# Gated recurrence and max-out MoE on one core: the orders of units 1 and 2 redrawn, the small sums first, one hid group ahead of the state's output

## Chip, core and metric

The kernel runs on one core of a Trainium2 chip. The metric is the device time of an execution in microseconds (us); smaller is better. Nine runs of the kernel before gave a median of 156.73 us, from 155.72 to 158.37.

## What is computed

Two layers follow each other. The first is a gated linear recurrence for each batch b and head h, with a 48 x 48 state that decays by alpha along its rows; the second is a max-out MLP on the recurrence's output, with all heads of a token side by side.

```python
# B, H, S, D = 4, 8, 768, 48
state = zeros((B, H, D, D))
for t in range(S):
    state = alpha[:, :, t, :, None] * state + einsum('bhd,bhe->bhde', k[:, :, t], v[:, :, t])
    y[:, :, t] = einsum('bhd,bhde->bhe', q[:, :, t], state)

x = y.transpose(0, 2, 1, 3).reshape(B * S, H * D)      # 3072 x 384
g = maximum(x @ w1, x @ w2)                            # 3072 x 1024
out = g @ w_out                                        # 3072 x 384
```

## The kernel before

**Units.** Time is cut into six chunks of 128 steps, and the four batches into two pairs. A unit u is one chunk of one pair, so there are 12 units; u and u-2 are neighbours in time for the same batches. Each unit has two halves, bb = 0 and 1, one for each batch of its pair.

**The recurrence of a unit.** Within a chunk the recurrence is done with matmuls. With L the running sum of log alpha in the chunk, counted from its middle:

- `ln(u)` takes the logarithm of alpha on ScalarE (ACT, L160) into `lg`.
- `sums(u)` adds up on TensorE: four matmuls against a triangular mask `mc` (L181, 384 columns, each on 64 rows, that is K=64) give L for both halves in two PSUM tiles `cs`; eight small matmuls against `halves` (L184, 4 columns, on 128 rows) give `dps`, the sums over the halves of the chunk, in spare columns of the first `cs` tile.
- `expm`, `expp` and `expd` (together `exps`) are ACT's exponentials: exp(-L) into `Em` (L197), exp(L) in place (L202), the chunk's decay `de` (L207).
- `kmul` makes k exp(-L) on GpSimd (POOL, L232), `qmul` makes q exp(L) on VectorE (DVE, L236, `qn`), `vcast` casts v to 16 bits on POOL (L169). `scale(u, bb)` is these three for one half.
- `turn(u, bb)` transposes kn and qn of one half on TensorE (L243) and copies them out on DVE (L245, `qk`).
- `kv(u)` is the chunk's own state (L259), added on DVE to the carried state `sb` into `tm` (L267; L269 for the first chunk); `state(u)` decays `tm` of unit u-2 into `sb` on POOL.
- `pairs(u, bb)` multiplies q with k of one half (L279, on 48 rows), and DVE applies the triangular mask while it copies out (L281, `pt`): two instructions for each half, called masks below.
- For units 0 and 1, whose carried state is zero, `yfirst` makes the output of one half (L327), evicted on ACT (`xn`, L333), and `xfirst` transposes it (L340) and copies it out on DVE (`xt`, L341). From unit 2 on `ystate` adds the part from the carried state (L291, 16 matmuls on 48 rows), `yin` the part within the chunk (L303), and `xturn` transposes.

**The MLP of a unit.** `hid(u, f2)` is one of four groups of six matmuls of 256 columns (L352); its relu into `gT` is done by ACT (L357), for the last group by DVE (L359). The weights are prepared so that w2's part goes straight to the output: `outp(u, n)` has three matmuls against `w2o` (L368) and eight against `w_out` (L370) for one half, an eviction on ACT (L373), and after both halves an output DMA issued by ACT (L378).

**Order.** The order of the calls is written out by hand under a manual schedule: each engine runs its instructions in the order of the Python calls. The first two units are written out one by one (from L424); from unit 2 on, a loop (from L509) interleaves unit u's recurrence, unit u-1's MLP and the preparation of unit u+1. `dummies(n)` are n matmuls on zeros (L416) whose result is not used.

**Buffers and loads.** PSUM has four tiles of tag `g`, two of `m` (hid, outp, dummies) and two of `pp` (pairs). Inputs have four buffers each and are loaded by SyncE (SP), in the order of the calls `load(u)`: two DMAs for alpha (L68) and three for k, q and v (L80). ACT's output DMAs share the DMA engines with these loads.

Of the kernel before, what the change touches and what calls it, by code (L numbers as in the profile page):

```python
# [15 lines left out]
def kernel(  # L16
# [22 lines left out]
    nc = tc.nc  # L39
    B, H, S, D = q.shape  # L40
# [69 lines left out]
    mc = constp.tile([128, 2, C], FP16)  # L110
    nc.gpsimd.memset(mc, 1.0)
    for bb in range(2):
        r = slice(64 * bb, 64 * bb + 64)
# [5 lines left out]
        r = slice(64 * bb, 64 * bb + 32)  # L119
# [30 lines left out]
    def pair(t, j):  # L150
        return t[:, 2 * j : 2 * j + 2, :].rearrange("p h w -> p (h w)")
# [5 lines left out]
    def ln(u):  # L157
        X = st[u]
        X["lg"] = LG[u % NB]
        nc.scalar.activation(  # L160
            out=X["lg"][:, :, :, 0:D], in_=X["af"].rearrange("p h j d -> p j h d"), func=ACTF.Ln
        )

    def vcast(u, bbs=(0, 1)):
        X = st[u]
        if 0 in bbs:
            X["v16"] = gp.tile([128, 2, H, D], FP16, tag="v16", name="v16")
        e = slice(bbs[0], bbs[-1] + 1)
        nc.gpsimd.tensor_copy(out=X["v16"][:, e], in_=X["vf"][:, e])  # L169

    def sums(u):
        X = st[u]
        c, g = divmod(u, NG)
        lg = X["lg"]
        cs = [new("g", [128, 512], FP32, 4, "cs") for _ in range(2)]
        X["csv"] = csv = [x[:, 0 : H * D].rearrange("p (h d) -> p h d", h=H) for x in cs]
        dps = cs[0][:, H * D : H * D + 4 * HP].rearrange("p (j b n) -> p j b n", j=HP, b=2)
        for j in range(2):
            for bb in range(2):
                r = slice(64 * bb, 64 * bb + 64)  # L180
                nc.tensor.matmul(csv[bb], lhsT=mc[r, j], rhs=lg[r, j, :, 0:D], start=(j == 0), stop=(j == 1))  # L181
        for hp in range(HP):
            for j in range(2):
                nc.tensor.matmul(  # L184
                    dps[:, hp], lhsT=pair(lg[:, j], hp), rhs=halves, start=(j == 0), stop=(j == 1)
                )
        X["dps"] = dps
        X["qn"], X["kn"], X["Em"] = [], [], []
        for bb in range(2):
            X["qn"].append(QN[(2 * u + bb) % (2 * NB)])  # L190
            X["kn"].append(KN[(2 * u + bb) % (2 * NB)])
# [7 lines left out]
    def expp(u, bb):  # L199

        X = st[u]
        nc.scalar.activation(out=X["csv"][bb], in_=X["csv"][bb], func=ACTF.Exp)  # L202
# [6 lines left out]
    def exps(u):  # L209
        for bb in range(2):  # L210
            expm(u, bb)
            expp(u, bb)
        expd(u)
# [24 lines left out]
    def turn(u, bb):  # L238
        X = st[u]
        tp = new("g", [128, 2, HP, C], FP16, 4, "tp")  # L240
        for n, src in ((1, X["kn"][bb]), (0, X["qn"][bb])):
            for j in range(HP):
                nc.tensor.transpose(tp[:, n, j, :], pair(src, j), ident)  # L243
        qk = gp.tile([128, 2, HP, C], FP16, tag="qk", name="qk")
        nc.vector.tensor_copy(out=qk, in_=tp)  # L245
        X["qk", bb] = qk
# [24 lines left out]
    def pairs(u, bb):  # L271
        X = st[u]
        qk = X["qk", bb]
        pt = X["pt", bb] = gp.tile([128, 2, HP, C], FP16, tag="pt", name="pt")
        pa = [new("pp", [128, HP, C], FP32, 2, "pp") for _ in range(2)]
        for j in range(HP):
            for a in range(2):
                r = slice(64 * a, 64 * a + D)
                nc.tensor.matmul(pa[a][:, j, :], lhsT=qk[r, 1, j, :], rhs=qk[r, 0, j, :], start=True, stop=True)  # L279
        for a in range(2):  # L280
            nc.vector.tensor_mul(out=pt[:, a], in0=pa[a], in1=u16.unsqueeze(1).to_broadcast([128, HP, C]))  # L281

    def ystate(u):
        X = st[u]
        X["ya"] = ya = [new("g", [128, 2, HP, D], FP32, 4, "ya") for _ in range(2)]
        X["begun"] = begun = set()
        for bb in range(2):
            for j in range(HP):
                for a in range(2):
                    r = slice(64 * a, 64 * a + D)  # L290
                    nc.tensor.matmul(  # L291
                        ya[a][:, bb, j, :], lhsT=X["qk", bb][r, 0, j, :], rhs=X["sb"][r, bb, j, :],
                        start=a not in begun, stop=False,
                    )
                    begun.add(a)
# [39 lines left out]
    def xfirst(u, bb):  # L335
        X = st[u]
        xp = new("g", [128, ND, C], FP16, 4, "xb")
        xf = X["xn"][:, bb].rearrange("p j a d -> p (j a d)")
        for ds in range(ND):
            nc.tensor.transpose(xp[:, ds, :], xf[:, ds * 128 : (ds + 1) * 128], ident)  # L340
        nc.vector.tensor_copy(out=X["xt"][:, :, bb, :], in_=xp)  # L341

    def hid(u, f2):
        X = st[u]
        if f2 == 0:
            X["gT"] = mp.tile([128, NF, 2 * C], FP16, tag="gT", name="gT")
        gT = X["gT"]
        hp = new("m", [128, 2, 2 * C], FP32, 2, "hp")
        for n in range(2):
            f = 2 * f2 + n  # L350
            for ds in range(ND):
                nc.tensor.matmul(  # L352
                    hp[:, n, :], lhsT=w12[:, ds, f * 128 : (f + 1) * 128],
                    rhs=X["xt"][:, ds].rearrange("p n t -> p (n t)"), start=(ds == 0), stop=(ds == ND - 1),
                )
        if f2 != 3:
            nc.scalar.activation(out=gT[:, 2 * f2 : 2 * f2 + 2, :], in_=hp, func=ACTF.Relu)  # L357
        else:
            nc.vector.tensor_relu(out=gT[:, 2 * f2 : 2 * f2 + 2, :], in_=hp)  # L359

    def outp(u, n):
        X = st[u]
        c, g = divmod(u, NG)
        if n == 0:
            X["outs"] = mp.tile([128, 2, DM], FP32, tag="outs", bufs=2, name="outs")
        op = new("m", [128, DM], FP32, 2, "op")
        for ds in range(ND):
            nc.tensor.matmul(op, lhsT=X["xt"][:, ds, n, :], rhs=w2o[:, ds, :], start=(ds == 0), stop=False)  # L368
        for f in range(NF):
            nc.tensor.matmul(  # L370
                op, lhsT=X["gT"][:, f, n * C : (n + 1) * C], rhs=wo16[:, f, :], start=False, stop=(f == NF - 1)
            )
        nc.scalar.copy(out=X["outs"][:, n, :], in_=op)  # L373
        dst = out.rearrange("(b s) d -> s b d", b=B)[c * C : (c + 1) * C, 2 * g : 2 * g + 2, :]
        if u == NU - 1:
            nc.scalar.dma_start(out=dst[:, n], in_=X["outs"][:, n])
        elif n == 1:
            nc.scalar.dma_start(out=dst, in_=X["outs"])  # L378
# [34 lines left out]
    def dummies(n):  # L413
        warm = new("m", [128, 512], FP32, 2, "warm")
        for _ in range(n):
            nc.tensor.matmul(warm, lhsT=wz[:, 0:128], rhs=wz, start=True, stop=True)  # L416

    def scale(u, bb):
        kmul(u, bb)
        qmul(u, bb)  # L420
        vcast(u, (bb,))
# [49 lines left out]
    hid(0, 2)  # L471
    expm(1, 1)
    expp(1, 1)
    hid(0, 3)
    expd(1)
    scale(1, 0)
    outp(0, 0)
    turn(1, 0)
    kv(1, (0,))
    outp(0, 1)  # L480
    pairs(1, 0)
    load(4)
    scale(1, 1)
    turn(1, 1)
    kv(1, (1,))
    yfirst(1, 0)
    dummies(1)
    pairs(1, 1)
    xfirst(1, 0)
    ln(2)  # L490
    dummies(2)
    yfirst(1, 1)
    sums(2)
    exps(2)
    xfirst(1, 1)
    for bb in range(2):
        kmul(2, bb)
    state(2)
    for f2 in range(4):
        hid(1, f2)  # L500
    for bb in range(2):
        qmul(2, bb)
    vcast(2)
    load(5)
    turn(2, 0)
    turn(2, 1)


    for u in range(2, NU):  # L509
        nxt = u + 1 < NU  # L510
        pairs(u, 0)
        kv(u)
        if nxt:
            ln(u + 1)
        if u > 2:
            hid(u - 1, 0)
            hid(u - 1, 1)
        else:
            outp(1, 0)
        if nxt:  # L520
            sums(u + 1)
            exps(u + 1)
            for bb in range(2):
                kmul(u + 1, bb)
            state(u + 1)
            vcast(u + 1)
        pairs(u, 1)
        ystate(u)
        if u > 2:
            hid(u - 1, 2)  # L530
            hid(u - 1, 3)
        if nxt:
            for bb in range(2):
                qmul(u + 1, bb)
        yin(u)
        outp(u - 1, 0 if u > 2 else 1)
        if nxt:
            turn(u + 1, 0)
        xturn(u)
        if nxt:  # L540
            turn(u + 1, 1)
        if u > 2:
            outp(u - 1, 1)
        if u + 4 < NU:
            load(u + 4)
# [34 lines left out]
```

## Time and profile before

| | |
|---|---|
| median of nine runs | 156.73 us |
| the profiled execution | 157.22 us, of it a span of 155.5 us |
| TensorE: busy with matmuls | 139.9 us (90% of the span), 1670 matmuls |
| VectorE | 93.0 us (60%) |
| ScalarE | 78.7 us (51%) |
| GpSimd | 47.4 us (30%) |
| DMA | 28.58 MB, mean 184 GB/s |
| granted TensorE clock | 1.000 |

The span runs from the first to the last instruction of the program; what the execution takes beyond it, 1.7 us, lies around the program. The chain that ended last puts 67% of the span on TensorE and 13% on SP's queue, the latter all in the first 21 us. In the loop one step takes about 10.15 us: sums of successive units start at 68.35, 78.51, 88.66 and so on.

How to read rows: a row of the timeline has start, duration, engine, line, operation, tiles and how many instructions it merges, and in brackets how long the engine was idle before it and what ended that. Rows of the chain have start, duration and place. A row of waits has the total in us, how often, and the longest. TensorE's instructions name the rows and columns of the array that they use, so 64*128 is on 64 rows.

### The profile page before, as it was taken

To read this page: it belongs to the slowest core of one execution; us is meant where nothing else is said; L and a number is where in the kernel's file an instruction comes from. 1 tells how busy PE (TensorE), PEld (TensorE's weight loads), DVE (VectorE), ACT (ScalarE), POOL (GpSimd) and SP (SyncE) were. 2 spreads that over 40 slices of the span, in tenths; PEclk is the share of its full clock that TensorE was granted. 3 is DMA by queue.
4 is the path that set the end of the run, shared out by engine and by line. 5 is a ranking of instruction groups with operands and counts; after the bars stand their busy time and mean duration, and the time that the engine had idled before them with its cause. 6 is when DMAs were issued, how large, how long until landed. Compare 5 with 4: busy or idle time off the path is not lost.

```text
span 155.5 us, 4085 instructions
## 1 busy us (share of the span) xinstructions
PE 139.9 (90%) x1670; PEld 96.4 (62%) x1670; DVE 93.0 (60%) x192; ACT 78.7 (51%) x165; POOL 47.4 (30%) x73
## 2 busy tenths in 40 slices
PE   6778868795769898999999999999999999999991
PEld 2236344563455577777777677786776777777660
DVE  5057814648449588676687684967867665654010
ACT  3375235813552668176293582853917629344421
POOL 6032320240260717209045081270530903500000
PEclk9999999999999999999999999999999999999999
DMA  3999999899999998999989999989989842020202
GB/s 85 195 383 212 364 220 315 153 202 241 202 187 185 189 222 191 194 232 195 201 213 199 188 243 212 190 205 201 242 168 210 208 90 103 4 101 0 94 11 101
DMA packets 93459, 28.58 MB, mean 184 GB/s; under 512 B 87424, under 2 KB 93056, under 8 KB 93440
## 3 DMA queue, kind: packets, MB, share of 16 engines
q1 hardware_dynamic: 90160, 23.60, 83.8%
q10 hardware_dynamic: 3280, 4.72, 8.8%
q8 instruction: 13, 0.21, 0.6%
q14 instruction: 6, 0.05, 0.1%
HBM read 23.59 MB, written 4.72 MB: 182 GB/s over the span
## 4 chain that ended last, share of the span: by engine, by line
PE 67%; SPq 13%; DVE 6%; ACT 5%; DMA 5%; issue 2%; ACTq 1%; DVEq 0%
PE op L370 20%; PE hp L352 16%; PE op L368 8%; PE tp L243 6%; SPq L80 5%; DMA w1f<-in_moe_w_dram 5%; PE pp L279 4%; SPq L103 3%; DVE pt L281 3%; PE kv L259 2%; PE ya L303 2%; PE cs L181 2%; PE xp L318 2%; SPq L68 2%; PE ya L291 2%
## 5 line engine op out<-in xcount | busy, mean ns | idle before, releaser
L232 POOL TENSOR_TENSOR kn<-kf,Em 128x384 f16<-128x384 f32 x24 | 23.6, 1001 | 77.4 <-ACT Em L197 65.7
L281 DVE TENSOR_TENSOR pt<-pp,u 128x512 f16<-128x512 f32 x48 | 30.9, 685 | 13.5 <-PE pp L279 12.6
L352 PE MATMUL hp<-xt,w 128*128 128x256 f16 x288 | 35.9, 273 | 2.2 <-DVE w L409 1.1
L370 PE MATMUL op<-wo,gT 128*128 128x384 f16 x192 | 35.1, 326 | 0.0
L373 ACT COPY outs<-op 128x384 f32<-128x384 f32 x24 | 11.5, 478 | 42.8 <-PE op L370 42.8
L352 PEld LDWEIGHTS <-w 128*128 128x128 f16 x288 | 26.5, 98 | 7.0 <-DVE w L409 2.1
L370 PEld LDWEIGHTS <-gT 128*128 128x128 f16 x192 | 18.8, 98 | 12.4
L245 DVE COPY qk<-tp 128x1024 f16<-128x1024 f16 x24 | 16.4, 687 | 12.7 <-PE tp L243 12.7
L357 ACT ACTIVATE gT<-hp 128x512 f16<-128x512 f32 x36 | 20.5, 594 | 4.5 <-PE hp L352 4.1
L359 DVE TENSOR_SCALAR gT<-hp 128x512 f16<-128x512 f32 x12 | 8.3, 692 | 12.7 <-PE hp L352 12.7
L236 DVE TENSOR_TENSOR qn<-qf,cs 128x384 f16<-128x384 f32 x24 | 12.3, 547 | 6.0 <-ACT de L207 6.0
L368 PE MATMUL op<-w2o,xt 128*128 128x384 f16 x72 | 15.6, 325 | 0.1
L160 ACT ACTIVATE lg<-af 128x768 f16<-128x768 f32 x12 | 10.1, 843 | 10.6 <-DMA af<-in_alpha_dram 6.9
L416 PE MATMUL warm<-wz 128*128 128x512 f16 x38 | 12.1, 446 | 1.3 <-DVE halves L123 1.3
L197 ACT ACTIVATE Em<-cs 128x384 f32<-128x384 f32 x24 | 11.7, 487 | 1.9 <-PE cs L184 1.7
L243 PE MATMUL tp<-ident,qn 128*128 128x128 f16 x96 | 9.3, 220 | 3.5 <-DVE qn L236 3.5
L202 ACT ACTIVATE cs<-cs 128x384 f32<-128x384 f32 x24 | 11.8, 490 | 0.0
L267 DVE TENSOR_TENSOR tm<-kv,sb 64x192 f32<-64x192 f32 x32 | 11.3, 352 | 0.5
L169 POOL CAST v<-vf 128x768 f16<-128x768 f32 (+1 forms) x14 | 10.2, 731 | 2.7 <-DMA vf<-in_v_dram 2.7
L279 PE MATMUL pp<-qk 48*128 48x128 f16 x192 | 9.6, 219 | 0.7 <-DVE qk L245 0.7
L243 PE MATMUL tp<-ident,kn 128*128 128x128 f16 x96 | 9.3, 220 | 0.3 <-POOL kn L232 0.3
L310 ACT CAST xn<-ya 128x384 f16<-128x384 f32 x20 | 8.6, 484 | 1.2 <-PE ya L303 0.7
(57 smaller groups left out, 140.9 us busy)
## 6 DMA issues: line engine op xcount, KB each, us to landing
af<-in_alpha_dram SPq DMA_DIRECT2D x24, 192.0 KB, 5.8
out_dram<-outs ACTq DMA_DIRECT2D x11, 384.0 KB, 4.9
kf<-in_k_dram SPq DMA_DIRECT2D x10, 384.0 KB, 6.2
qf<-in_q_dram SPq DMA_DIRECT2D x10, 384.0 KB, 7.5
vf<-in_v_dram SPq DMA_DIRECT2D x10, 384.0 KB, 6.6
w2f<-in_moe_w_dram SPq DMA_DIRECT2D x3, 512.0 KB, 5.3
wof<-in_moe_w_out_dram SPq DMA_DIRECT2D x2, 768.0 KB, 7.4
w1f<-in_moe_w_dram SPq DMA_DIRECT2D x4, 384.0 KB, 9.5
```

Source lines behind the costliest of these rows:

```text
L202: nc.scalar.activation(out=X["csv"][bb], in_=X["csv"][bb], func=ACTF.Exp)
L232: nc.gpsimd.tensor_mul(out=X["kn"][bb][:, :, 0:D], in0=X["kf"][:, bb], in1=X["Em"][bb])
L236: nc.vector.tensor_mul(out=X["qn"][bb][:, :, 0:D], in0=X["qf"][:, bb], in1=X["csv"][bb])
L243: nc.tensor.transpose(tp[:, n, j, :], pair(src, j), ident)
L245: nc.vector.tensor_copy(out=qk, in_=tp)
L279: nc.tensor.matmul(pa[a][:, j, :], lhsT=qk[r, 1, j, :], rhs=qk[r, 0, j, :], start=True, stop=True)
L281: nc.vector.tensor_mul(out=pt[:, a], in0=pa[a], in1=u16.unsqueeze(1).to_broadcast([128, HP, C]))
L352: nc.tensor.matmul(hp[:, n, :], lhsT=w12[:, ds, f * 128 : (f + 1) * 128], rhs=X["xt"][:, ds].rearrange("p n t -> p (n t)"), start=(ds == 0 ...
L357: nc.scalar.activation(out=gT[:, 2 * f2 : 2 * f2 + 2, :], in_=hp, func=ACTF.Relu)
L368: nc.tensor.matmul(op, lhsT=X["xt"][:, ds, n, :], rhs=w2o[:, ds, :], start=(ds == 0), stop=False)
L370: nc.tensor.matmul(op, lhsT=X["gT"][:, f, n * C : (n + 1) * C], rhs=wo16[:, f, :], start=False, stop=(f == NF - 1))
L416: nc.tensor.matmul(warm, lhsT=wz[:, 0:128], rhs=wz, start=True, stop=True)
```

## The change

No arithmetic changes and no instruction is added to a unit, except for one dummy matmul more in all.

1. In `sums` the eight small matmuls come ahead of the four on 64 rows.
2. In unit 1, `scale(1, 0)` goes ahead of hid(0,3) and `expd(1)`; turn and kv of half 0 go ahead of outp(0,0); `scale(1, 1)` goes ahead of pairs(1,0), so that q exp(L) of half 1 stands on VectorE ahead of the masks of half 0; outp(0,1) moves behind yfirst(1,0).
3. `ln(2)` goes ahead of xfirst(1,0), and `sums(2)` ahead of yfirst(1,1). One dummy ahead of pairs(1,1) goes, two are put ahead of xfirst(1,1).
4. Unit 2's v cast and q exp(L) go ahead of MoE 1 (the four groups hid(1,·)), and its two turns stand between groups of MoE 1 rather than behind all four.
5. In the loop, for u > 2, hid(u-1, 2) moves from behind `ystate(u)` to ahead of it, between it and `pairs(u, 1)`.

```diff
@@ sums
-        for j in range(2):
-            for bb in range(2):
-                r = slice(64 * bb, 64 * bb + 64)
-                nc.tensor.matmul(csv[bb], lhsT=mc[r, j], rhs=lg[r, j, :, 0:D], start=(j == 0), stop=(j == 1))
         for hp in range(HP):
             for j in range(2):
                 nc.tensor.matmul(
                     dps[:, hp], lhsT=pair(lg[:, j], hp), rhs=halves, start=(j == 0), stop=(j == 1)
                 )
+        for j in range(2):
+            for bb in range(2):
+                r = slice(64 * bb, 64 * bb + 64)
+                nc.tensor.matmul(csv[bb], lhsT=mc[r, j], rhs=lg[r, j, :, 0:D], start=(j == 0), stop=(j == 1))
@@ the written-out orders
     expm(1, 1)
     expp(1, 1)
+    scale(1, 0)
     hid(0, 3)
     expd(1)
-    scale(1, 0)
-    outp(0, 0)
     turn(1, 0)
     kv(1, (0,))
-    outp(0, 1)
+    outp(0, 0)
+    scale(1, 1)
     pairs(1, 0)
     load(4)
-    scale(1, 1)
     turn(1, 1)
     kv(1, (1,))
     yfirst(1, 0)
-    dummies(1)
+    outp(0, 1)
     pairs(1, 1)
+    ln(2)
     xfirst(1, 0)
-    ln(2)
+    sums(2)
     dummies(2)
     yfirst(1, 1)
-    sums(2)
     exps(2)
+    dummies(2)
     xfirst(1, 1)
     for bb in range(2):
         kmul(2, bb)
     state(2)
-    for f2 in range(4):
-        hid(1, f2)
+    vcast(2)
     for bb in range(2):
         qmul(2, bb)
-    vcast(2)
+    hid(1, 0)
+    hid(1, 1)
+    turn(2, 0)
+    hid(1, 2)
+    turn(2, 1)
+    hid(1, 3)
     load(5)
-    turn(2, 0)
-    turn(2, 1)
@@ the loop
         pairs(u, 1)
+        if u > 2:
+            hid(u - 1, 2)
         ystate(u)
         if u > 2:
-            hid(u - 1, 2)
             hid(u - 1, 3)
```

## The prediction

> **What bounds the kernel.** I read the page's 40 slices first, then the busy times by stage, then the waits of TensorE, and last the timeline of the stages that the change touches.
>
> ```profile
> PE   6778868795769898999999999999999999999991
> DMA  3999999899999998999989999989989842020202
> ```
>
> Each digit is a slice of 3.9 us. From about 56 us TensorE is full; until then it has holes, and the DMA engines are full until about 116 us.
>
> ```profile
> 28.66:36.00 7.34, 6.37 (x58) 4.09 (x56) 4.35 (x8) 2.99 (x8) 3.10 (x4) 1.00 1.19 189
> 36.00:46.00 10.00, 6.71 (x81) 4.62 (x81) 5.07 (x11) 5.03 (x11) 3.71 (x5) 1.00 1.21 215
> 46.00:56.00 10.00, 8.89 (x132) 6.16 (x132) 7.74 (x16) 4.48 (x11) 3.72 (x5) 1.00 1.10 176
> 66.00:76.00 10.00, 10.00 (x137) 7.42 (x135) 7.27 (x14) 5.87 (x13) 3.72 (x5) 1.00 1.19 209
> ```
>
> The first number is the length, the second TensorE's busy time. Up to 28.66 us the chain of waits stands on the DMA of w1, which the change doesn't touch. From there to 56 us TensorE is idle for 0.97 + 3.29 + 1.11 = 5.4 us; from 66 us it has no idle time, so only its own instructions count, and any lead won earlier is kept. The granted clock is 1.00 throughout.
>
> ```profile
> PE tp L243 <- DVE qn L236: 2.5, 2, 1.5
> PE yb L327 <- DVE pt L281: 0.6, 2, 0.4
> PE hp L352 <- DVE xt L341: 0.5, 1, 0.5
> PE ya L291 <- DVE tm L267: 0.4, 1, 0.4
> ```
>
> Largest of these are two transposes that wait for q exp(L): 1.5 us in unit 1 and 1.0 in unit 2. The last row is the wait in front of ystate(3).
>
> **The orders of units 1 and 2.** I laid the new queues end to end with this trace's durations. hid(0,3) ends at 30.5 as before, on the weights. On DVE, qn(1,0) now goes ahead of the relu: DVE is free at 29.62, and q lands between k (29.4) and v (31.0) by the rows below, so I take 30.6 for its end. Behind it the relu ends at 31.2 instead of 31.24, the qk copy (0.69) at 31.85. turn(1,0) then takes 30.5 to 31.05, and kv(1,0) waits for the cast of v, which waits for a DMA:
>
> ```profile
> 31.04 0.50 POOL L169 CAST v<-vf 128x384 f16<-128x384 f32 x1 [0.56 <-DMA vf<-in_v_dram]
> 34.84 0.50 POOL L169 CAST v<-vf 128x384 f16<-128x384 f32 x1 [1.47 <-DMA vf<-in_v_dram]
> ...
> 46.17 0.84 ACT L160 ACTIVATE lg<-af 128x768 f16<-128x768 f32 x1 [1.26 <-DMA af<-in_alpha_dram]
> ...
> 55.82 0.84 ACT L160 ACTIVATE lg<-af 128x768 f16<-128x768 f32 x1 [0.83 <-DMA af<-in_alpha_dram]
> ```
>
> So kv(1,0) starts at 31.58, a new wait of 0.5, with outp(0,0) queued behind it: 31.75 to 33.54 (0.49 + 1.30 by the chain). pairs(1,0) ends at 33.9; the masks follow at 34.05 to 35.35, if qn(1,1), now ahead of them, has run: its q lands between k (32.4) and v (34.8), by even spacing at 33.4, so it ends at 33.95. At the late end the masks would start at 35.4 and everything behind would be 1.3 later. turn(1,1) is done at 34.45. kv(1,1) waits for the second cast (35.34) until 35.38, a new wait of 0.9; where this order hides nothing, the old one had the cast done 1.77 ahead of its use at 37.11. Then yfirst(1,0) to 35.75, outp(0,1) to 37.54, pairs(1,1) to 37.9, xfirst(1,0) to 38.2. On ACT the evicted outp(0,1) (0.48) and its DMA issue (0.38) stand ahead of ln(2): it runs from 38.57 to 39.41, where it ran at 38.05. sums(2) waits for it and ends at 40.07 (before: about 40.9).
>
> Now the dummies: those behind sums(2) are on the path, two of 0.22 and a change of tile shape, 0.5 in all. yfirst(1,1) starts at 40.59, its eviction xn ends at 41.46, and the exponentials stand behind xn on ACT: 41.38, where the first ran at 41.17. hid(1,0) starts at 42.30 against 41.72. At this point the new order is 0.6 *behind*.
>
> It wins in what follows. The old one did four hid groups, then stood through qn (1.0), qk (0.5) and the masks. Now: hid(1,0) and (1,1) to 43.61; qn(2,0) follows the last exponential (43.14) and ends at 43.73; turn(2,0) to 44.05, hid(1,2) to 44.70, turn(2,1) to 45.14, hid(1,3) to 45.80, with both qk copies beside hid groups. pairs(2,0) and kv(2) end at 46.72, and outp(1,0), at 48.04 before, starts there: **1.3 us ahead**. Its relu, behind the qk copies on DVE, ends at 46.7, ahead of its use at 48. load(4) and load(5) keep their place among SP's issues, since SP waits here for earlier DMAs, not for compute; POOL keeps its order too.
>
> **The sums, small ones first.** TensorE pays when it goes from instructions on 128 rows to those on 64 or 48 and back:
>
> ```profile
> 97.57 1.31 PE hp L352 x12
> 98.88 0.43 PE cs L181 x4
> 99.31 0.28 PE cs L184 x8
> 99.60 0.33 PE pp L279 x8
> 99.93 0.33 PE ya L291 x16
> 100.26 1.42 PE hp L352 x12
> ```
>
> This is the chain in one step of the loop. Twelve hid matmuls cost 1.31 behind kv (128 rows) and 1.42 behind ya: an edge costs 0.11. The other edges give 0.07 to 0.1 by the start times. There are four: hid to cs, cs to the small sums L184, these to pp, ya to hid. With the small sums first the middle two become one. In unit 2, where no hid follows, this saves two edges, 0.18: the lead there is 1.5.
>
> **hid(u-1,2) between pairs and ystate.** Here a rule speaks against the change. The Trainium skill's page "TensorEngine Tiling (Array Packing)", section Key Properties, says that a change of tiling mode drains TensorE. Setting 128-row hid between two 48-row groups adds two edges, exactly those that the sums save (four against four); by the rule alone the loop gains nothing. The rows show what the rule leaves out:
>
> ```profile
> 58.74 0.18 PE L291 MATMUL ya<-sb,qk 48*128 48x48 f16 x1
> 59.35 0.37 PE L291 MATMUL ya<-sb,qk 48*128 48x48 f16 x15 [0.42 <-DVE tm L267]
> ...
> 99.76 0.18 PE L291 MATMUL ya<-sb,qk 48*128 48x48 f16 x1
> 99.89 0.37 PE L291 MATMUL ya<-sb,qk 48*128 48x48 f16 x15
> ```
>
> The second ya matmul waits for the last tm. In unit 3 that costs 0.60; in later units 0.12 (99.89 against 99.77), too short for the list of waits. hid(2) takes 0.66, so it covers both. From the end of hid(u-1,1) to yin the new order needs 0.21 small sums, 0.08 edge, 0.34 cs, 0.23 pp, 0.10 edge, 0.66 hid, 0.10 edge, 0.22 ya, 0.09 edge, 0.66 hid = 2.69. Unit 3 took 57.70 to 60.97, 3.27: gain 0.6. Units 4 to 9, 2.80 each: 6 x 0.11 = 0.7. Unit 10 has no tm: nothing. Unit 11 has no sums either and gets two edges more: -0.2. What is late next: the masks, which start 0.1 earlier behind tm (1.29 long) and leave yin 0.15; and lg, which ends just as hid ends, so that the small sums may wait up to 0.05 for it.
>
> **What the lead runs into.** The alpha of unit 4 starts lg at 55.82, on its DMA; sums(4) can then start at 56.71. It ran at 57.80 behind an edge of 0.1, so with a lead of 1.5 it is due at 56.2 and stalls 0.5. Later loads have more room: unit 5's lg started on the eviction, not on its DMA. The write of unit 1's output is issued 1.5 earlier too. The skill's page "DMA: Bandwidth & Descriptors", section Queues, rings and completion order, says that a DMA engine takes turns between queues: sharing evenly for the 1.8 us left to alpha would add 0.9. By the row, a write of this size lands 4.9 after its issue, so most of it falls behind alpha. I take 0 and keep 0.9 for the range.
>
> **Sum.** 1.5 - 0.5 + 0.6 + 0.7 - 0.2 = 2.1. The profiled execution took 157.22 with a span of 155.5; it would take 155.1 (span 153.4). It lay 0.5 above the median 156.73, so I forecast 154.6.
>
> **Rivals.** *The lead is lost to DMA*: alpha of unit 4 comes as late as sums(4) ran before, or v(1,1) comes 1.5 later. For it: the full DMA row and three rows above that wait on landings. Against: 0.5 of the 1.5 is counted already. Gain 0.6 + 0.7 - 0.2 = 1.1: 155.6. *The lead is kept whole*: the 0.83 in front of lg was partly the DMA issue ahead of it on ACT, and alpha was there. Gain 2.6: 154.1. *Edges decide, and it is slower*: in front of and behind the lone hid group a matmul may have to run out at its full 273 ns (mean of L352) rather than 0.10. Two such edges in nine steps are 18 x 0.175 = 3.2 more: 157.8. It breaks even at 0.22 an edge. For it: the rule above, and that this edge (pp to hid) isn't in the loop of before; against: hid to cs is, at 0.10.
>
> **Chances.** Forecast 0.57 (153.8 to 155.4), lead lost 0.22, lead kept 0.12, slower 0.09. A measurement tells 0.5% (0.8 us) from no change. Faster by that takes the first and third and two thirds of the second, less the tail of the first: 0.81; the same 0.11; slower 0.08. The range goes from the kept lead with 1.0 of scatter (the runs before spread 2.6), 153.1, to the lost lead with 0.6, 156.2.
>
> **What would show it.** hid(1,0) later than 41.72 but outp(1,0) near 46.7; waits of kv for the casts of v; lg of unit 4 at 55.3 to 55.9 with sums(4) right behind; no tm in front of ya; a step of the loop of about 10.04 instead of 10.15. I am wrong if v of unit 1 lands later than here, or if steps grow.

## The result and the profile after

The changed kernel takes **155.34 us** (median of 16 runs, 153.95 to 156.76), and the kernel before, run beside it, 157.16 us (53 runs). The ratio is 0.9892, with a 95% interval of 0.9865 to 0.9919: 1.7 us less, between 1.3 and 2.1. Its profiled execution took 154.9 us with a span of 153.2, against 157.22 and 155.5 before: 2.3 us less. Ratios here and below, and the medians of part 4, leave out executions that took over 1.5% longer than the fastest of the same kernel, single ones of 200 us and more among them.

In `sums` the small matmuls are now L180 and the four on 64 rows L186; the other lines are as before. The page's slices, 3.8 us each, have fewer holes in the tenth and twelfth, and the DMA engines are full to about the same point as before (the 33rd slice here, the 32nd there, so to about 125 us):

```profile
PE   6678896788699899999999999999999999999991
DMA  3999999799999899997999999999998992020202
```

and the busy times by stage (length, then TensorE, its weight loads, VectorE, ScalarE, GpSimd, and the clock):

```profile
28.66:36.00 7.34, 6.08 (x65) 3.96 (x66) 5.88 (x11) 2.73 (x8) 3.10 (x4) 1.00 1.17 187
36.00:46.00 10.00, 8.05 (x89) 5.44 (x86) 4.72 (x11) 5.63 (x12) 3.72 (x5) 1.00 1.21 213
46.00:56.00 10.00, 9.53 (x140) 7.03 (x139) 8.23 (x17) 5.36 (x12) 3.72 (x5) 1.00 1.11 181
66.00:76.00 10.00, 10.00 (x138) 7.42 (x136) 7.21 (x16) 5.78 (x14) 3.78 (x5) 1.00 1.12 205
```

In the first stage TensorE idles 0.29 us more than before (1.26 against 0.97); in the next two it idles 1.95 and 0.47 where it was 3.29 and 1.11. That is the shape that was forecast: first a debt, then the gain. The longest of TensorE's waits from 28 to 62 us that the change touches (total, how often, longest):

```profile
PE cs L180 <- ACT lg L160: 1.4, 1, 1.4
PE kv L259 <- POOL v L169: 0.7, 2, 0.5
PE hp L352 <- DVE xt L341: 0.4, 1, 0.4
```

The waits for q exp(L) (2.5 us before) and for tm are gone. kv now waits for the casts of v, and sums(2) for its logarithm; the wait for xt, 0.5 before, stays. The casts and the logarithms of units 2 to 4:

```profile
31.13 0.50 POOL L169 CAST v<-vf 128x384 f16<-128x384 f32 x1 [0.58 <-DMA vf<-in_v_dram]
34.38 0.50 POOL L169 CAST v<-vf 128x384 f16<-128x384 f32 x1 [1.14 <-DMA vf<-in_v_dram]
...
38.72 0.84 ACT L160 ACTIVATE lg<-af 128x768 f16<-128x768 f32 x1 [0.56 <-ACT outs L373]
46.35 0.84 ACT L160 ACTIVATE lg<-af 128x768 f16<-128x768 f32 x1 [0.64 <-DMA af<-in_alpha_dram]
54.84 0.84 ACT L160 ACTIVATE lg<-af 128x768 f16<-128x768 f32 x1 [1.30 <-DMA af<-in_alpha_dram]
```

The last row differs from the forecast: alpha of unit 4 let its logarithm start at 54.84, not at 55.82 as before. One step of the loop, in the chain of waits (start, duration, place):

```profile
95.32 1.31 PE hp L352 x12
96.63 0.19 PE cs L180 x8
96.82 0.43 PE cs L186 x4
97.25 0.23 PE pp L279 x8
97.48 0.76 PE hp L352 x6
98.24 0.30 PE ya L291 x16
98.55 0.76 PE hp L352 x6
99.31 0.40 PE ya L303 x16
```

The small sums fell from 0.28 to 0.19, the pairs behind them from 0.33 to 0.23 and ya from 0.33 to 0.30, while hid's 1.42 behind ya is split into two times 0.76. From the sums to the end of hid that is 2.67 instead of 2.79. By the starts of outp in successive steps, one step takes 10.060 us where it took 10.153.

### The profile page after: what moved, and what is told of

Read it like the earlier page. It is cut to its first block, busy times and chain, and to the rows that moved or that the text cites. A ratio compares the mean times of both kernels' runs of the same rounds, so it can differ in the third digit from the quotient of the medians.

```text
span 153.2 us, 4086 instructions
## 1 busy us (share of the span) xinstructions
PE 139.4 (91%) x1671; PEld 96.1 (63%) x1671; DVE 93.2 (61%) x192; ACT 78.6 (51%) x165; POOL 47.5 (31%) x73
## 4 chain that ended last, share of the span: by engine, by line
PE 71%; SPq 16%; DMA 3%; ACT 3%; DVE 2%; issue 1%; ACTq 1%; POOL 0%
PE op L370 20%; PE hp L352 19%; PE op L368 8%; SPq L80 8%; PE tp L243 6%; SPq L103 4%; PE pp L279 4%; DMA vf<-in_v_dram 3%; PE cs L186 3%; PE kv L259 3%; PE ya L303 3%; PE xp L318 2%; SPq L68 2%; PE ya L291 2%; DVE pt L281 2%; PE cs L180 1%
## 5 line engine op out<-in xcount | busy, mean ns | idle before, releaser
L352 PE MATMUL hp<-xt,w 128*128 128x256 f16 x288 | 37.7, 273 | 1.8 <-DVE w L409 1.1
L352 PEld LDWEIGHTS <-w 128*128 128x128 f16 x288 | 25.7, 98 | 7.5 <-DVE w L409 2.3
L279 PEld LDWEIGHTS <-qk 48*128 48x128 f16 x192 | 6.2, 94 | 6.1 <-issue 3.4
```

The source lines that it names most:

```text
L352: nc.tensor.matmul(hp[:, n, :], lhsT=w12[:, ds, f * 128 : (f + 1) * 128], rhs=X["xt"][:, ds].rearrange("p n t -> p (n t)"), start=(ds == 0 ...
```

## The experiments

Medians are over all of a kernel's own runs (part 4 apart); ratios are to the kernel before on the same chip, whose medians were 157.31, 157.88 and 156.92 us in the three sets of runs that follow. "Step" is the time between two outp(·, 0) in the loop (the middle one of units 4 to 9), from the trace, and "lead-in" the time from hid(0,3) to outp(1,0). Spans of profiled executions can't be compared directly: hid(0,3), which starts when the DMAs of w1 are in, started anywhere from 28.56 to 30.24 us in the profiled executions.

| kernel | median us | ratio [95%] | step us | lead-in us |
|---|---|---|---|---|
| before | 157.16 | | 10.153 | 18.36 |
| changed kernel | 155.34 | 0.9892 [0.9865, 0.9919] | 10.060 | 17.05 |
| only the small sums first | 156.04 | 0.9950 [0.9915, 0.9984] | 10.087 | 18.25 |
| only hid(u-1,2) moved | 156.70 | 0.9974 [0.9948, 1.0001] | 10.167 | 18.37 |
| both, orders as before | 155.73 | 0.9933 [0.9902, 0.9964] | 10.069 | 19.87 |
| only the orders redrawn | 156.30 | 0.9949 [0.9919, 0.9978] | 10.160 | 17.07 |

**1. The change taken apart.** Four kernels carry one or two of its three parts.

The small sums alone:

```diff
@@ sums of the kernel before
+        (the eight matmuls on halves)
         (the four matmuls on 64 rows)
-        (the eight matmuls on halves)
```

> Only the small sums go first; all else as before. The forecast's account: in the loop two edges between 128 and 64 rows go (about 0.18 us a step), but the last tm on VectorE keeps its time, so the second ya matmul only waits longer (about 0.3 instead of 0.12) and the step stays at 10.15; units 2 and 10, where no tm holds ya, gain 0.1 to 0.2 each. In all 0.2 to 0.4 us faster than before. Rival, edges alone count: 0.18 in each of nine steps, 1.6 us faster, and a step of about 9.97.

Measured: 0.995, and a step of 10.087. The 0.8 us is twice what was expected, and half of the rival's 1.6. The wait in front of ya grew as expected, to about 0.3. In this kernel's chain (start, duration, place) the tm instructions of VectorE end, and the last 15 ya follow:

```profile
97.58 0.35 DVE tm L267
...
97.94 0.37 DVE tm L267
...
98.36 0.37 PE ya L291 x15
```

So saved edges did bring nothing ahead of ya, and still the step fell by 0.066. This was the first sign that the step doesn't end where the prediction looked. In the trace of before, yin's last matmul starts 7.046 us into a step (counted from the first matmul of outp(u-2,1)), and outp(u-1,0) at 7.139, just behind the relu of hid(u-1,2) on ScalarE, which ended at 7.089. Here yin stands where it did, but with two edges fewer in the sums the exponentials start 0.095 earlier, and the relu behind them ends at 7.001; outp starts at 7.074, right behind yin.

hid(u-1,2) alone:

```diff
         pairs(u, 1)
+        if u > 2:
+            hid(u - 1, 2)
         ystate(u)
         if u > 2:
-            hid(u - 1, 2)
             hid(u - 1, 3)
```

> Only hid(u-1,2) goes ahead of ystate; sums as before. The forecast's account: two edges more in each step (0.19) against a wait on tm of 0.12 that goes: steps of units 4 to 9 get 0.07 longer, unit 3 gains 0.4, units 10 and 11 lose 0.2 each; in all 0.3 to 0.5 us slower than before, with a step of about 10.22. Rival, the cover is what counts and edges are nearly free: 1.3 us faster.

This missed: where 0.3 to 0.5 us more was expected, it is 0.4 less, with an interval from 0.8 less to none, and the step grew by 0.013 only. The rival's 1.3 us less is excluded too. Its chain:

```profile
98.25 0.33 PE pp L279 x8
98.58 0.76 PE hp L352 x6
99.34 0.31 PE ya L291 x16
99.65 0.76 PE hp L352 x6
100.41 0.40 PE ya L303 x16
```

yin does start 0.08 later in the step. By the starts of the matmuls the wait for tm, 0.124, is gone, and each added edge costs 0.097 (0.149 from the last matmul of pairs to hid, where pairs to ya took 0.052; 0.205 from hid to ya, where hid to hid takes 0.109). But outp no longer waits for the relu: that ends where it did, within 0.01, and yin now ends behind it, which gave 0.067 of the 0.08 back. The slower rival, with 0.22 or more for an edge, is excluded.

Both, with the orders of before:

```diff
@@ the two edits above together
```

> Small sums first and hid(u-1,2) ahead of ystate together, the orders of units 1 and 2 as before. The forecast's account: 0.2 in unit 2, 0.6 in unit 3, 0.1 in each of six steps, minus 0.2 in unit 11: 1.2 us faster than before, with a step of 10.06. If the two edits simply added up, this would be the sum of the two runs with one of them each, by the account about 0.

Measured: 0.9933, about 1.05 us of the 1.2 expected, and a step of 10.069 (two of the six took 10.10 and 10.13). Whether the two edits help each other can't be told from the times, since the two alone add up to 0.8 + 0.4 = 1.2 as well. The steps tell it: -0.066 and +0.013 alone, -0.084 together. Its lead-in of 19.87 is not the kernel's order: TensorE's clock fell in that one execution (last section).

Only the redrawn orders:

```diff
@@ the changed kernel, with sums and the loop as before
```

> Only the redrawn orders of units 1 and 2. The forecast's account: outp(1,0) starts 1.3 us earlier than before, nothing else; with the stall on the alpha of unit 4 the lead is cut to 0.8 to 1.3 us. Rival, the lead is lost to DMA: sums(4) starts as late as before (57.8) and the time is the same within 0.3.

Measured: 0.9949, or 0.8 us, and a lead-in of 17.07: 1.29 shorter than before, like the changed kernel's. The wait of ya for tm in unit 3 is still 0.606. The whole lead reached sums(4), which came 26.84 us after hid(0,3) instead of 28.11, without a stall; 0.29 was lost late, in a step of 10.34 whose outp waited for the relu. The parts add: 1.05 + 0.8 = 1.85 against 1.7 in all. A rival for part of the 0.8 is the clock. Among executions under 160 us with a mean granted clock of 0.995 or more, the mean time falls by 0.6 us with the redrawn orders (156.19 against 156.76) and by 1.3 with both loop edits (155.49); below that clock lay 4 of 21 with the redrawn orders, but 29 of 73 of the kernel before. So some of the 0.8 may come from rarer falls of the clock; with this scatter it is not shown.

**2. What a lead of the first units is worth.** Three kernels change the written-out part of the changed kernel.

```diff
@@ no dummies behind sums(2)
     sums(2)
-    dummies(2)
     yfirst(1, 1)
```

> The changed kernel without the two dummies behind sums(2). If they are on the path, as the forecast has it, yfirst(1,1) and hid(1,0) start 0.5 us earlier than in the changed kernel, and the time falls by 0.3 to 0.5 us against it, unless the loads of unit 4 take it back (then 0 to 0.2). If they lie beside a wait, nothing moves.

It missed: 155.79 us, 0.9886 [0.9849, 0.9923], no better than with them. In its trace yfirst(1,1) starts 0.71 us behind the start of sums(2), where it was 1.16: the dummies are on the path, at about the price that was forecast (0.45 of 0.5). But then, at 40.9 us, the clock fell, and the lead-in of 18.16 tells more of that than of the dummies. The granted clocks of all executions point the same way. Of the 16 without these dummies 9 had a mean clock of 0.989 or less (median 155.95 us; the other 7, 154.99), against 1 of 18 of the three other kernels in this set. So the dummies seem to prevent such falls; but the changed kernel itself had 6 of 17 in the runs of the result, and where in an execution a fall lies is known from its profile only (with the relu early, in part 4, it lay at 7.7 us, ahead of all this), so this is not shown.

```diff
@@ the logarithm of unit 2 earlier
     yfirst(1, 0)
+    ln(2)
     outp(0, 1)
     pairs(1, 1)
-    ln(2)
```

> The changed kernel with ln(2) called ahead of outp(0,1), so that on ScalarE it no longer stands behind that eviction and its DMA issue. sums(2) starts about 0.95 us earlier than in the changed kernel and so does hid(1,0). If loads don't limit, the time falls by 0.9 us against the changed kernel; if they do (sums(4) can't start before its alpha, about 56), only by 0.3 to 0.5, and TensorE shows a wait on lg in front of sums(4) of about 0.5.

Measured: 155.69 us, 0.9890 [0.9827, 0.9953]. The lead-in fell to 16.47, 0.58 less; but sums(4) then stood behind its logarithm, and that behind alpha's DMA (timeline, ScalarE and TensorE):

```profile
55.52 0.84 ACT L160 ACTIVATE lg<-af 128x768 f16<-128x768 f32 x1 [2.48 <-DMA af<-in_alpha_dram]
...
54.44 1.47 PE L352 MATMUL hp<-xt,w 128*128 128x256 f16 x12
56.42 0.35 PE L180 MATMUL cs<-halves,lg 128*128 128x4 f16 x8 [0.51 <-ACT lg L160]
```

The whole 0.58 is lost there: from hid(0,3) to sums(4) it is 26.59, in the changed kernel 26.50. The ratio, with its wide interval, shows none of the 0.3 to 0.5 us that were expected for this case.

```diff
@@ no output DMA for units 0 and 1 (those rows are not written)
-        elif n == 1:
+        elif n == 1 and u > 1:
```

> The changed kernel without the output DMAs of units 0 and 1 (their rows of the output aren't written), so that the loads of units 2 to 5 share the DMA engines with nothing. If loads hold back the usual execution of the changed kernel around sums(4), it is 0.3 to 0.6 us faster than the changed kernel; if they don't, the same within 0.2.

Measured: 154.79 us, 0.9842 [0.9799, 0.9885]. By the ratios that is 0.8 us less than the changed kernel in the runs of the result, but the intervals overlap. The lead-in is 16.40: ln(2) stands behind no DMA issue on ScalarE, and TensorE waits 0.7 for it instead of 1.4. sums(4) did not wait (the logarithm ended at 55.35, sums(4) began at 55.73), so here the lead, 0.66 at sums(4), reached the loop. From there to the end it took 97.42 us against 96.95, so 0.48 of it was lost again in this execution, 0.29 of that in one late step of 10.35 in which sums(11) waited for its logarithm. Both the place on ScalarE and the traffic were changed at once; how much each gave is not separated.

**3. The last step.** For unit 11 hid(10,2) goes behind ystate again:

```diff
         pairs(u, 1)
-        if u > 2:
+        if nxt and u > 2:
             hid(u - 1, 2)
         ystate(u)
         if u > 2:
+            if not nxt:
+                hid(u - 1, 2)
             hid(u - 1, 3)
```

> The changed kernel with hid(10,2) behind ystate again in the last step alone, where there are no sums. By the price of two edges it is 0.2 us faster than the changed kernel, at the end of the trace: from the first hid matmul of that step to yin 3.27 instead of 3.49 us. If edges cost nothing, the same.

Measured: 155.17 us, 0.9865 [0.9804, 0.9926]; from outp(9,0) to outp(10,0) 8.904 us against 9.117. Without sums and tm in that step, this is the plainest price of two edges: 0.213, or 0.107 each. In this execution sums(4) waited 0.6 for its logarithm.

**4. What the step ends on.** ScalarE and TensorE at the end of one step of the changed kernel (start, duration):

```profile
97.35 0.49 ACT L197 ACTIVATE Em<-cs 128x384 f32<-128x384 f32 x1
97.73 0.49 ACT L202 ACTIVATE cs<-cs 128x384 f32<-128x384 f32 x1
98.14 0.48 ACT L197 ACTIVATE Em<-cs 128x384 f32<-128x384 f32 x1
98.52 0.49 ACT L202 ACTIVATE cs<-cs 128x384 f32<-128x384 f32 x1
98.92 0.19 ACT L207 ACTIVATE de<-cs 128x16 f32<-128x16 f32 x1
98.98 0.61 ACT L357 ACTIVATE gT<-hp 128x512 f16<-128x512 f32 x1
...
99.14 0.56 PE L303 MATMUL ya<-v,pt 128*128 128x48 f16 x16
99.64 0.65 PE L368 MATMUL op<-w2o,xt 128*128 128x384 f16 x3
```

ScalarE is busy without a gap from the first exponential on. The relu of hid(u-1,2), whose matmuls end at 98.24 by the chain, is last in its queue and ends at 99.59; outp takes the PSUM tile (tag `m`, two of them) that this relu gives free, and starts at 99.64. Its weights and xt have long been there. The test moves the relu ahead of the last two exponentials:

```diff
             sums(u + 1)
-            exps(u + 1)
+            expm(u + 1, 0)
+            expp(u + 1, 0)
+            expm(u + 1, 1)
             for bb in range(2):
                 kmul(u + 1, bb)
-            state(u + 1)
-            vcast(u + 1)
         pairs(u, 1)
         if u > 2:
             hid(u - 1, 2)
+        if nxt:
+            expp(u + 1, 1)
+            expd(u + 1)
+            state(u + 1)
+            vcast(u + 1)
         ystate(u)
```

> The changed kernel, but in the loop ScalarE runs the relu of hid(u-1,2) ahead of the last exponential exp(L) of half 1 and the decay de, instead of behind them. Theory: a step now ends on ScalarE's chain, because outp takes the PSUM tile that this relu gives free (it ends 6.995 us after the step's start, outp follows at 7.046). With the relu at about 5.9 to 6.5, outp starts when yin ends, at about 6.96: the step goes from 10.06 to 9.97 us, 0.7 us over eight steps, and the ratio to the kernel before falls from 0.989 to about 0.985. Rival 1: the masks or tm on VectorE bind the step, then outp stays near 7.05 and the step at 10.06. Rival 2: the later exponential delays q exp(L), xn or the state, and the step grows beyond 10.06.

```profile
97.34 0.48 ACT L197 ACTIVATE Em<-cs 128x384 f32<-128x384 f32 x1
97.71 0.59 ACT L357 ACTIVATE gT<-hp 128x512 f16<-128x512 f32 x1
98.18 0.50 ACT L202 ACTIVATE cs<-cs 128x384 f32<-128x384 f32 x1
98.59 0.20 ACT L207 ACTIVATE de<-cs 128x16 f32<-128x16 f32 x1
...
98.34 0.56 PE L303 MATMUL ya<-v,pt 128*128 128x48 f16 x16
98.74 0.65 PE L368 MATMUL op<-w2o,xt 128*128 128x384 f16 x3
```

In the changed kernel outp started 0.50 after yin's first matmul, here 0.40 after it, and the relu has ended before. The step is 9.967, as forecast: the 0.093 was ScalarE's order. In the times of whole executions it is not to be seen: 154.51 us, 0.9858 [0.9812, 0.9904], while the changed kernel, run beside it, had 154.74:

> The changed kernel itself, on the same chip as the three runs beside it: it takes part as their yardstick. A ratio of 0.989 to the kernel before again, within its interval of 0.9865 to 0.9919. The profiled execution also tells whether sums(4) waits for the logarithm in the changed kernel: by the theory it does where alpha lands late (up to 0.5 us, as forecast) and does not where alpha lands as in the first profile.

Measured: 0.9869 [0.9827, 0.9910], the first result again. In this execution the logarithm of unit 4 started at 54.95 and sums(4) waited 0.17 for it, between the first profile's nothing and the 0.6 to 1.0 of others. One step more was late, 10.22, since q exp(L) waited for the DMA of q. From sums(4) to the end the two kernels take 97.18 (96.95 in the first profile) and 96.22 us by the trace, 0.7 to 1.0 less; the medians differ by 0.2. Each ratio is uncertain by 0.7 us, so with five and six executions the times neither show this gain nor contradict it.

The relu and the last step together:

```diff
@@ both edits
```

> The run with the early relu, and in the last step hid(10,2) behind ystate(11) again as in the kernel before. Theory: the two gains add, step 9.97 us and the last step 0.2 shorter: about 0.9 us less than the changed kernel, a ratio of about 0.983 to 0.984. Rival: with no sums in the last step the early relu has nothing to gain there, and the last step's 0.2 is there as before; if the steps do not shorten, only 0.2 us and a ratio of 0.988.

Measured: 154.41 us, 0.9838 [0.9795, 0.9882]; steps of 9.966 and 9.967 but for two of 9.976 and 10.010, and a last step of 8.904. From sums(4) to the end it takes 96.05 us, 1.1 less than the changed kernel beside it and 0.9 less than in the first profile, as expected; the medians differ by 0.3.

With the logarithm of unit 2 early as well:

```diff
@@ the kernel above, and ln(2) ahead of outp(0, 1)
```

> As the run before, and ln(2) ahead of the eviction and the output DMA of outp(0,1) on ScalarE. Theory (the alpha of unit 4 limits what a lead is worth): outp(1,0) comes 0.58 us earlier after hid(0,3), sums(4) then waits for the logarithm by about the same, and the end is where it is without the edit, within 0.2 us. Rival: the lead is kept, and the time is 0.5 us below the run before, a ratio near 0.980.

Measured: **153.24 us**, 0.9776 [0.9731, 0.9820], the best of all, and the only one whose interval lies clear of that of the changed kernel beside it. Its profile:

```profile
54.37 0.84 ACT L160 ACTIVATE lg<-af 128x768 f16<-128x768 f32 x1 [2.99 <-DMA af<-in_alpha_dram]
...
52.95 1.47 PE L352 MATMUL hp<-xt,w 128*128 128x256 f16 x12
55.27 0.35 PE L180 MATMUL cs<-halves,lg 128*128 128x4 f16 x8 [0.84 <-ACT lg L160]
```

The expectation missed: by the times the rival, with a ratio near 0.980, is nearer. As the theory had it, sums(4) waits for alpha, about 1.0 us. What it had wrong is that no room was left in front of alpha. In the run before, the logarithm of unit 4 ended at 55.19 and sums(4) began at 55.88; here they stand at 55.21 and 55.27. So of the 1.79 us by which outp(1,0) starts earlier than in that run (44.64 against 46.43; 0.26 of it an earlier hid(0,3)), the trace keeps 0.6 at sums(4) and at the end. The other half of the 1.2 us between the two medians is open. Against the changed kernel beside it the trace gives 1.1 us, from hid(0,3) to the end, and the medians 1.5.

## Why the prediction was right

The forecast was 2.1 us less; the ratio says 1.7, and the two profiled executions 2.3. In the latter the terms can be read one by one. That the sum came so near is in part luck: the stall of 0.5 was not there, and the other terms gave 0.3 less than forecast.

- **The lead of the redrawn orders, 1.5.** Measured 52.53 - 51.07 = 1.46 at outp(1,1). The debt came as forecast, hid(1,0) at 42.50 (forecast 42.30), and so did its repayment, outp(1,0) at 46.79 (46.72). kv waited 0.46 and 0.26 for the casts of v, where 0.5 and 0.9 were expected: the second v landed earlier than before.
- **The stall on alpha of unit 4, -0.5.** In the first profile it is 0, since alpha's logarithm started 0.98 earlier than before, which nothing in the prediction said. The runs show it as a quantity that varies: 0.17 in a second execution of the same kernel, 0.6 in the one with the last step put back, none in the two with the relu early, 0.7 and 1.0 us where ln(2) goes early (counted from 1.31 behind the start of hid's twelve matmuls, where sums(4) follows if nothing waits). The mechanism holds, but 0.5 was too much for the usual execution. "Later loads have more room" was wrong for one of them: in the second execution q of unit 4 was late by 0.14. What moves alpha's landing is not settled. Where its logarithm waited for the DMA, it started 25.1 to 26.2 us after hid(0,3), in no order by kernel; without two output DMAs it was 24.6, the earliest, but those DMAs weren't removed alone.
- **Unit 3, 0.6.** Measured 0.61 up to yin (3.27 to 2.66), of which outp then lost 0.10 to the relu.
- **Units 4 to 9, 6 x 0.11.** Measured 6 x 0.093 = 0.56. The step that failed is "what is late next": the prediction named the masks and lg, and it was ScalarE's queue. yin did come 0.12 earlier in a step, and outp kept 0.093 of it. outp already waited 0.067 for the relu in the kernel before, and waits 0.093 in the changed one (both counted beyond the 0.026 from the start of yin's last matmul to outp in the kernels where nothing waits). The trace of before showed it: in each step, in rows of the timeline like the first three, and once, at unit 10, in the chain that ended last.

```profile
101.33 0.61 ACT L357 ACTIVATE gT<-hp 128x512 f16<-128x512 f32 x1
101.52 0.56 PE L303 MATMUL ya<-v,pt 128*128 128x48 f16 x16
101.98 0.65 PE L368 MATMUL op<-w2o,xt 128*128 128x384 f16 x3
...
131.82 0.49 ACT gT L357
132.35 0.65 PE op L368 x3
```

But such a wait is too short for the list of waits, and outp's other inputs were so early that I didn't look at which buffer it takes. For the same reason the split of this term was wrong, as the expectations of the first two runs show: the small sums alone were to bring nothing until hid moves and gave 0.066, through ScalarE; hid alone was to cost 0.07 and cost 0.013.
- **Unit 11, -0.2.** Measured 8.90 to 9.117, -0.21.
- **The price of an edge.** 0.097 and 0.107 by the two kernels that isolate it, where 0.07 to 0.11 was taken. The rule that a change of tiling mode drains TensorE (the Trainium skill, "TensorEngine Tiling (Array Packing)", Key Properties) is borne out in sign; at this size it doesn't decide. The slower rival needed 0.22.
- **Two slips without effect.** The DMA row of before is full to its 32nd slice, about 124 us, not 116. The relu of hid(0,3), 0.69 long behind qn's 30.6, comes to 31.3, not 31.2; it ended at 31.30.

Together: 1.46 + 0.51 + 0.56 - 0.21 = 2.3. The ratio's 1.7 is less, and part of the distance can be told. From hid(0,3) to the end the kernel before took 125.82 us and the changed one 123.45, but 123.86 in its second profiled execution, with the stall of 0.17 and the late q: 2.0 less. That execution lies at the median of its set. What remains is within the ratio's interval; the executions that weren't profiled can't be looked into.

## What to carry to other kernels

Where an engine has no idle time in the loop, a shorter sequence on it gains only until the next engine's queue order binds; so follow each instruction's buffer, not only its data, to the last reader that gives it free, and see what stands ahead of that reader in its queue. A lead won in a stage fed by DMA is worth what the next load's landing leaves of it, and that varies from execution to execution. Test the parts of a change singly even when the sum comes out: here two of the parts gained for reasons other than those forecast.

## What the hardware showed beside

In two of the profiled executions TensorE's clock fell to half between 36 and 46 us. Busy times by stage of the kernel without the dummies (columns as above), and in the second fence a row of the timeline of the kernel with both loop edits and the old orders:

```profile
36.00:40.00 4.00, 2.71 (x33) 1.53 (x30) 2.24 (x6) 1.78 (x3) 0.00 (x0) 1.00 1.00 164
40.00:45.00 5.00, 4.47 (x40) 2.88 (x41) 1.40 (x4) 2.76 (x8) 2.67 (x4) 0.66 1.15 248
```

```profile
41.44 4.12 PE L352 MATMUL hp<-xt,w 128*128 128x256 f16 x24 [0.45 <-DVE xt L341]
```

In the first, the clock is at 0.5 from 40.9 us for 3.4 us, after a stretch in which TensorE was busy for two thirds of the time and never idle for more than 1.4 us; in the second from 37.0 us for 6.8 us, after an idle time of 1.5 us, and 24 hid matmuls took 4.12 us where 12 take 1.47. The Trainium skill ("TensorE: Matmul & The Clock Gate", Part 1: The HAM clock gate) puts such a fall down to an idle window of about 3.4 us. The lengths of the falls are one and two such windows, but no idle time here came near one. The changed kernel, with an idle time of 1.4 us at the same place, and the kernel before, with 1.5, kept their full clock there. What sets off such a fall is not shown.
